# A fifth early group of attention weights, made by GpSimd as powers of two during the first MoE

## The chip, the cores and the metric

One core of one Trainium2 chip. The metric is the device time of one execution in microseconds (us), and lower is better. Each ratio below is the mean time of one kernel's fast runs over the mean of the fast runs of the kernel before in the same rounds on the same chip. It is therefore not quite the ratio of the medians that are quoted beside it.

## The reference

```python
def _attn_ref(q, kv, w_sr):            # q (4, 12288, 128), kv (4, 384, 32, 128)
    kv_pool = kv.reshape(B, H // 4, 4, W // 4, 4, C).mean(axis=(2, 4))
    k = v = kv_pool.reshape(B, -1, C) @ w_sr          # 768 keys a batch
    s = scale * (q @ k.transpose(0, 2, 1))
    a = np.exp(s - s.max(-1, keepdims=True))
    a /= a.sum(-1, keepdims=True) + 1e-09
    return a @ v
def _moe_ref(x, w_in, w_out):          # 49152 tokens, d_ff 2048
    h = x @ w_in
    return (h * (1.0 / (1.0 + np.exp(-1.702 * h)))) @ w_out
```

The attention's output is the MoE's input, token by token.

## The kernel before

Tokens are handled in 96 groups of 512. The first 48 pass through attention and then the MoE, and then the other 48 do the same. Per group, attention needs six chunks (128 keys x 512 queries) of exponentials and the MoE 16 chunks of the activation. A chunk is a matmul into PSUM, then a ScalarE activation into a ring of chunks in SBUF, then a second matmul that reads the ring. ScalarE takes three chunks in one instruction.

While the first MoE runs, VectorE has time to spare. The kernel lets it make the attention weights of four groups of the *second* attention ahead of time, as a polynomial of ten steps. They rest in reserved rows at the start of the ring.

```python
EARLY = 4
AG = 102                                   # chunks in the ring, reserved rows included
def early_exp(ps, out):                    # ten VectorE steps for one chunk
    nc.vector.tensor_scalar(a, ps, scale / LN2, -126.0, MUL, MAX)        # PSUM -> SBUF
    nc.vector.tensor_scalar(b, a, 127.0, MAGIC, MIN, ADD)                # SBUF -> SBUF
    nc.vector.tensor_scalar(e, b, MAGIC - 127.0, 2.0 ** 23, SUB, MUL)    # SBUF -> SBUF
    nc.vector.scalar_tensor_tensor(b, b, MAGIC, a, SUB, SUB)             # two SBUF inputs
    nc.vector.tensor_scalar_mul(a, b, COEFFS[5])                         # SBUF -> SBUF
    for k in (4, 3, 2, 1):
        nc.vector.scalar_tensor_tensor(a, a, COEFFS[k], b, ADD, MUL)     # two SBUF inputs
    nc.vector.scalar_tensor_tensor(out, a, COEFFS[0], e.bitcast(F32), ADD, MUL)
    # ... (yields between the steps cut)
```

The keys of batches 2 and 3 (counted from 0, so batch 3 is the fourth) are pooled by accumulating DMAs, issued from GpSimd's queue. A "gate" times those DMAs. It is a memset on VectorE followed by a memset of the same tile on GpSimd, so GpSimd issues no DMA before VectorE gets there.

```python
def gate():
    nc.vector.memset(gate_tile, 0.0)
    nc.gpsimd.memset(gate_tile, 0.0)
# ...
for b, lo in ((2, 2), (3, 24)):            # g: the group that the first MoE is at
    if lo <= g < lo + 8:
        gate()
        add_kv(b, g - lo)                  # two accumulating DMAs from GpSimd's queue
    if g in (lo + 10, lo + 12):
        use_kv(b, (g - lo - 10) // 2)      # VectorE adds the two halves, then keys and values
```

The softmax here doesn't subtract the row's maximum and nothing guards it: scores larger than these inputs give would overflow.

Of the kernel before, what the change touches and what calls it, by code (L numbers as in the profile page):

```python
# [7 lines left out]
F32 = mybir.dt.float32  # L8
# [6 lines left out]
MUL = mybir.AluOpType.mult  # L15
# [3 lines left out]
MAX = mybir.AluOpType.max  # L19
MIN = mybir.AluOpType.min  # L20
EQ = mybir.AluOpType.is_equal


@with_exitstack
def kernel(
    ctx, tc, q, kv, w_sr, moe_w_in, moe_w_out, out,
):
    nc = tc.nc
# [5 lines left out]
    JC = J // 128  # L34
    d_ff = moe_w_in.shape[1]
    FCH = d_ff // 128
    scale = 1.0 / (C ** 0.5)
    G = 512
# [3 lines left out]
    GB = NG // B  # L42
# [15 lines left out]

    R = 2
    XS = NS // R  # L60
    EARLY = 4
    AG = 102

    cpool = ctx.enter_context(tc.tile_pool(name="const", bufs=1))
    xpool = ctx.enter_context(tc.tile_pool(name="x", bufs=1))
# [5 lines left out]
    npool = ctx.enter_context(tc.tile_pool(name="norm", bufs=3))  # L71
# [9 lines left out]
    free = {6: 0.0, 7: 0.0}  # L81
    last_acc = 7

    def acc(key=None):

        nonlocal last_acc
        last_acc = next_acc()
        if key:
            closes[last_acc] = key
        return banks[:, last_acc, :]  # L90

    def next_acc():
        return min((m for m in (13 - last_acc, last_acc) if m not in closes), key=lambda m: free[m])
# [19 lines left out]
    kv_tiles, kv_sums, pooled, pTs, kTs, vs = {}, {}, {}, {}, {}, {}  # L113
# [83 lines left out]
    qTs = {}  # L197
# [58 lines left out]
    for m in range(0, 128, 32):  # L256
        p = slice(m, m + 32)
        nc.vector.tensor_tensor(ident[p, p], row[p], col[p], EQ)
        if m > 0:
# [16 lines left out]

    ag = agpool.tile([128, AG, 512], BF, name="ag")
    wide = cpool.tile([128, 16, 32], F32R)
# [12 lines left out]
    slot_of = {}  # L291
    head, low = 8 * JC, 0

    def place(chunks):
        nonlocal head
        if chunks[0][0] == "a" and chunks[0][1] < 8:
# [3 lines left out]
            return ag[:, lo[0]:lo[-1] + 1:JC, :]  # L300
        if head + len(chunks) > AG:
            head = low
# [9 lines left out]
    def room_ahead():  # L312
        busy = set(slot_of.values())
        return next((n for n in range(AG - low) if (head - low + n) % (AG - low) + low in busy), AG - low)

    early = range(NG // R, NG // R + EARLY)

    def weights(c):
        if c[0] == "a" and c[1] in early:
            return ag[:, (c[1] - early[0]) * JC + c[2], :]  # L320
        return ag[:, slot_of[c], :]
# [47 lines left out]
    LN2 = 0.6931471805599453  # L369
# [11 lines left out]
    def early_step():  # L381
        nonlocal steps
        on_dve(next(steps))
        if steps.gi_frame.f_locals["last"]:
            steps = None
            made.add(early_todo.pop(0))

    def early_exp(ps, out):
# [18 lines left out]
        last = True  # L407
        yield 3.5

    made = set()  # L410
    steps, early_todo = None, [(i, jc) for i in early for jc in range(JC)]

    def turn(w):

# [23 lines left out]
    av_of, xt_of, turns = {}, {}, []  # L438
# [33 lines left out]
    def background_moe(g):  # L472
# [7 lines left out]
        if g == 12:  # L480
            low = EARLY * JC
            head = max(head, low)
# [18 lines left out]
    extras = []  # L501
# [34 lines left out]
    seq, todo = [], []  # L536
    todo_early = [("a", t, a) for t in range(NT) for a in range(2) if (t // TS * TS + TS - 1) // 4 in early]
# [25 lines left out]
    def prepare(p):  # L563
# [10 lines left out]
        for i, _ in part:  # L574
# [25 lines left out]

    FIXED, CHUNK, SWITCH, HANDOVER, EVACUATE, LATE = 0.33, 1.975, 6.0, 1.0, 4.5, 1.0
    COST = {pool_chunk: (2.5, 2.0), key_chunk: (0.7, 2.0), value_chunk: (0.7, 2.0),
            transpose_q: (1.2, 4.0), early_fill: (1.0, 5.5), key_and_value: (1.0, 3.0),
            transpose_pooled: (1.5, 3.0), make_k: (1.0, 3.0), make_v: (1.5, 3.0), turn: (1.5, 3.5)}
    SMALL, TURN = 0.27, 5.5
    PAUSE = 4.0
    now, end, extra_at = 0.0, [], 0.0
    source, dve = None, 0.0

    def on_dve(cost):  # L610
        nonlocal dve
        dve = max(dve, now + 1.0) + cost


    def fill(p):
        nonlocal now
        if p >= len(seq):
            return
        kind, part = seq[p]
        prepare(p)  # L620
        lo = K * (p % 2)
        (fill_attn if kind == "a" else fill_moe)(part, banks[:, lo:lo + len(part), :])
        if p >= 2:
            now = max(now, end[p - 2] + HANDOVER / 2)
        now += len(part)
        begin = max(now + HANDOVER / 2, end[p - 1] if p else 0.0)
        if p and kind != seq[p - 1][0]:
            begin += SWITCH
        end.append(begin + FIXED + CHUNK * len(part))
# [3 lines left out]
    for n in range(len(seq)):  # L633
        fill(n + 2)
        while True:
            room = room_ahead()
            limit = end[-1] - K - HANDOVER if n + 3 < len(seq) else 1e9
            bank = free[next_acc()]
            f = None
            if turns and max(now, bank) >= turns[0][0]:  # L640
                f, args = turn, turns[0][1:]
            if f is None and extras and now >= max(extra_at, bank):
                f, *args = extras[0]
            if steps and dve <= now + 2.0:
                early_step()
            if not f and not steps and early_todo and low and min(slot_of.values()) >= low and (2, 1) in vs and dve <= now + 2.0 and now >= bank:
                f, args = early_fill, early_todo[0]
            if f and max(now, bank) + COST[f][0] > limit + (LATE if f is turn else 0.0 if f is early_fill else 4.5) and room >= 4 * K:
                f = None
            if f:  # L650
                now = max(now, bank) + COST[f][0]
                f(*args)
                free[last_acc] = dve + 1.0 if f is early_fill else now + COST[f][1]
                if f in (transpose_pooled, make_k, make_v):
                    on_dve(2.5)
                extra_at = max(now + PAUSE, dve + 1.5 if f in (transpose_pooled, make_k, make_v) else 0.0)
                if f is turn:
                    turns.pop(0)
                elif f is early_fill:
                    pass  # L660
                else:
                    extras.pop(0)
                continue
            if not source:

                if todo_early and all((i, jc) in made for t in range(todo_early[0][1], todo_early[0][1] + TS)
                                      for i in [t // 4] for jc in range(JC)):
                    source = todo_early
                else:
                    source = todo  # L670
            if not source:
                break
            kind, i, c = source[0]
            needs = at[("at" if kind == "a" else kind, i, c)]
            cost = K * SMALL if kind == "a" else 1.0
            first_of = c == 0 and (kind == "m" or i % TS == 0)
            if source is not todo_early and (needs > n or (kind == "a" and first_of and at["at", i + TS - 1, 1] > n)
                                             or (kind == "a" and i // 4 in early and (i // 4, JC - 1) not in made)):
                if first_of:
                    source = None  # L680
                break
            start = now if source is todo_early else max(now, end[needs] + HANDOVER)
            if first_of:
                start = max(start, bank)
            if start + cost > limit and not (room < 2 * K + 1 or (room < 4 * K and start == now)):
                if first_of:
                    source = None
                break
            now = start + cost
            (drain_attn if kind == "a" else drain_moe)(i, c)  # L690
            source.pop(0)
            if not todo_early:
                low = 0
            if c == (1 if kind == "a" else FCH - 1) and (kind == "m" or i % TS == TS - 1):
                source = None
    assert not todo and not todo_early and not turns and not extras and not early_todo


# [28 lines left out]
```

## Time and profile before

| | before |
|---|---|
| time | 971.72 us median of 3 (971.57 to 972.06) |
| span of the profiled run | 969.9 us, granted TensorE clock 0.999 |
| TensorE / ScalarE busy | 947.4 / 946.2 us |
| VectorE / GpSimd busy | 344.3 / 66.1 us |
| first MoE, from the 10th group on (255 to 490 us) | TensorE 233.4, ScalarE 232.3, VectorE 173.0, GpSimd 22.5 of 235 us |

Three rows of the page's slices are added here. The span is cut into 40 equal slices, and a digit is the busy share of a slice in tenths.

```profile
PE   7899999999999999999999999999999999999997
...
POOL 3100100330000242000000000000000000000000
PEclk9999999999999999999999999999999999999999
```

TensorE is busy for 90% or more of every slice from the third to the last but one. GpSimd (POOL) is nearly empty, and that emptiness is what the change wants to use.

### The profile page before, as it was taken

To read this page: it belongs to the slowest core of one execution; us is meant where nothing else is said; L and a number is where in the kernel's file an instruction comes from. 1 tells how busy PE (TensorE), PEld (TensorE's weight loads), DVE (VectorE), ACT (ScalarE), POOL (GpSimd) and SP (SyncE) were. 2 spreads that over 40 slices of the span, in tenths; PEclk is the share of its full clock that TensorE was granted. 3 is DMA by queue.
4 is the path that set the end of the run, shared out by engine and by line. 5 is a ranking of instruction groups with operands and counts; after the bars stand their busy time and mean duration, and the time that the engine had idled before them with its cause. 6 is when DMAs were issued, how large, how long until landed. Compare 5 with 4: busy or idle time off the path is not lost.

```text
span 969.9 us, 15710 instructions
## 1 busy us (share of the span) xinstructions
PE 947.4 (98%) x6243; PEld 508.4 (52%) x6359; DVE 344.3 (35%) x734; ACT 946.2 (98%) x705; POOL 66.1 (7%) x113
## 2 busy tenths in 40 slices
PE   7899999999999999999999999999999999999997
PEld 3567777644444444454445777754444444444443
DVE  4444333211578778778312333320110110101010
ACT  4999999999999999999999999999999999999997
POOL 3100100330000242000000000000000000000000
PEclk9999999999999999999999999999999999999999
DMA  9897861999852799224429976562222222222222
GB/s 182 161 196 150 113 96 34 109 159 171 173 107 33 102 155 113 40 36 78 77 44 155 193 142 121 110 131 43 44 33 44 44 33 44 40 37 40 37 33 44
DMA packets 354169, 89.70 MB, mean 92 GB/s; under 512 B 328048, under 2 KB 351728, under 8 KB 353776
## 3 DMA queue, kind: packets, MB, share of 16 engines
q1 hardware_dynamic: 323936, 56.06, 34.2%
q0 software_dynamic: 29104, 32.51, 21.9%
q8 instruction: 49, 0.80, 0.3%
q10 hardware_dynamic: 1056, 0.13, 0.1%
q14 instruction: 24, 0.20, 0.1%
HBM read 52.49 MB, written 45.88 MB: 101 GB/s over the span
## 4 chain that ended last, share of the span: by engine, by line
PE 80%; ACT 16%; issue 2%; DVE 1%; DMA 1%; POOL 0%; POOLq 0%
PE banks L515 27%; PE banks L508 26%; ACT ag L510 14%; PE banks L340 14%; PE banks L329 11%; ACT ag L331 2%; DVE qT L230 1%; DMA x<-in_kv_dram 1%; PE banks L377 1%; PE banks L419 0%; PE banks L134 0%; PE banks L224 0%; DVE xt L357 0%; PE banks L271 0%; DVE o_sb L523 0%
## 5 line engine op out<-in xcount | busy, mean ns | idle before, releaser
L510 ACT ACTIVATE ag<-banks 128x1536 bf16<-128x1536 f32 x512 | 691.1, 1512 | 2.9 <-PE banks L508 2.2
L515 PE MATMUL banks<-ag,w_out_sb 128*128 128x512 bf16 x1523 | 410.1, 379 | 2.9 <-ACT ag L510 0.5
L508 PE MATMUL banks<-x,w_in_sb 128*128 128x512 bf16 x1478 | 406.0, 378 | 2.0 <-ACT ag L510 0.4
L331 ACT ACTIVATE ag<-banks 128x1536 bf16<-128x1536 f32 (+1 forms) x188 | 249.4, 1481 | 11.2 <-PE banks L329 10.8
L515 PEld LDWEIGHTS <-w_out_sb 128*128 128x128 bf16 x1536 | 149.8, 98 | 179.9 <-issue 1.0
L508 PEld LDWEIGHTS <-w_in_sb 128*128 128x128 bf16 x1536 | 147.8, 97 | 174.0 <-issue 14.1
L523 DVE STREAM_TRANSPOSE o_sb<-banks 128x512 f32<-128x512 f32 x96 | 68.7, 716 | 395.6 <-PE banks L515 372.6
L340 PEld LDWEIGHTS <-ag 128*128 128x128 bf16 x2304 | 149.9, 97 | 48.1 <-issue 1.6
L340 PE MATMUL banks<-v,ag 128*128 128x129 bf16 x2304 | 167.9, 220 | 0.7 <-DVE v L158 0.7
L329 PE MATMUL banks<-qT,kT 128*128 128x512 bf16 x507 | 146.3, 378 | 8.0 <-ACT ag L331 4.5
L349 DVE RECIPROCAL rec<-banks 128x3 f32<-128x3 f32 x128 | 23.0, 180 | 139.0 <-PE banks L340 138.9
L404 DVE SCALAR_TENSOR_TENSOR ea<-ea,eb 128x512 f32<-128x512 f32 x96 | 66.0, 687 | 2.8
L329 PEld LDWEIGHTS <-kT 128*128 128x128 bf16 x552 | 47.3, 97 | 34.6 <-issue 4.2
L357 DVE TENSOR_TENSOR x<-banks,rec 128x384 bf16<-128x384 f32 x104 | 57.9, 557 | 3.6
L166 POOL DMA_DIRECT2D kvs<-in_kv_dram x32 | 40.6, 1319 | 27.9 <-DMA kvs<-in_kv_dram 25.5
L444 POOL MEMSET gate_tile<- 1x8 f32 x38 | 3.8, 100 | 450.1 <-DVE gate_tile L443 450.1
L393 DVE TENSOR_SCALAR ea<-banks 128x512 f32<-128x512 f32 x24 | 16.6, 691 | 26.5 <-PE banks L377 26.5
L406 DVE SCALAR_TENSOR_TENSOR ag<-ea,ee 128x512 bf16<-128x512 f32 x24 | 16.5, 689 | 1.1
L399 DVE SCALAR_TENSOR_TENSOR eb<-eb,ea 128x512 f32<-128x512 f32 x24 | 16.5, 687 | 0.7
L357 DVE TENSOR_TENSOR xt<-banks,rec 128x384 bf16<-128x384 f32 x24 | 13.4, 557 | 0.8
L230 DVE COPY qT<-banks 128x512 bf16<-128x512 bf16 x15 | 9.8, 687 | 4.5 <-PE banks L224 4.4
L421 DVE COPY x<-banks 128x768 bf16<-128x768 bf16 x12 | 6.7, 557 | 11.7 <-PE banks L419 11.7
(65 smaller groups left out, 154.8 us busy)
## 6 DMA issues: line engine op xcount, KB each, us to landing
out_dram<-o_sb SPq DMA_DIRECT2D x382, 64.0 KB, 2.0
kvs<-in_kv_dram POOLq DMA_DIRECT2D x32, 384.0 KB, 6.4
q_bf<-in_q_dram POOLq DMA_DIRECT2D x20, 512.0 KB, 6.8
x_bf<-x SPq DMA_DIRECT2D x13, 768.0 KB, 5.6
x<-in_kv_dram POOLq DMA_DIRECT2D x12, 512.0 KB, 12.5
x<-in_q_dram POOLq DMA_DIRECT2D x3, 512.0 KB, 20.0
w_in_sb<-in_moe_w_in_dram POOLq DMA_DIRECT2D x1, 512.0 KB, 5.0
w_out_sb<-in_moe_w_out_dram POOLq DMA_DIRECT2D x1, 512.0 KB, 7.2
```

Source lines behind the costliest of these rows:

```text
L166: nc.gpsimd.dma_start(out=kv_sums[b][:, i2], in_=kv_p[b, i, w, :, i2], **({"accum_op": ADD} if n else {}))
L230: nc.vector.tensor_copy(dst, src)
L329: nc.tensor.matmul(ps[:, k, :], kTs[i // GB][:, jc * 128:(jc + 1) * 128], rhs, start=True, stop=True)
L331: nc.scalar.activation(place([("a",) + c for c in chunks]), ps, AF.Exp, scale=scale)
L340: nc.tensor.matmul(av_of[u][:, k * (C + 1):(k + 1) * (C + 1)], weights(("a", i, jc))[:, o:o + T], vs[i // GB][:, jc, 0:C + 1], start=(jc = ...
L349: nc.vector.reciprocal(rec, ps[:, :, C])
L357: nc.vector.tensor_tensor(to, ps[:, :, 0:C], rec.unsqueeze(2).broadcast_to([128, TS, C]), MUL)
L404: nc.vector.scalar_tensor_tensor(a, a, COEFFS[k], b, ADD, MUL)
L508: nc.tensor.matmul(ps[:, k, :], w_in_sb[:, fc * 128:(fc + 1) * 128], x[:, g % (4 * XS) * G:(g % (4 * XS) + 1) * G], start=True, stop=True)
L510: nc.scalar.activation(place([("m",) + c for c in chunks]), ps, AF.Gelu_apprx_sigmoid)
L515: nc.tensor.matmul(o_of[g], w_out_sb[:, fc, :], weights(("m", g, fc)), start=(fc == 0), stop=(fc == FCH - 1))
L523: nc.vector.transpose(o_sb, o_of.pop(g))
```

## The change

A fifth group's six chunks are made early too. TensorE writes the scores of a chunk to PSUM, VectorE scales them to y, and GpSimd computes 2 to the power y straight into the ring. In the second attention ScalarE then has six chunks of exponentials fewer. y has two buffers. The ring has 99 chunks in place of 102, and 30 of them are reserved in place of 24. In the kernel's own order planning a power costs POWER = 150 units.

```diff
-    EARLY = 4
-    AG = 102
+    EARLY = 5
+    BY_DVE = 4
+    AG = 99
# ...
+    def pow_fill(i, jc):
+        nonlocal pool
+        ps = acc()
+        rhs = qTs[i // 4][:, 0, (i % 4) * G:(i % 4 + 1) * G]
+        nc.tensor.matmul(ps, kTs[i // GB][:, jc * 128:(jc + 1) * 128], rhs, start=True, stop=True)
+        y = npool.tile([128, 512], F32, name="y", bufs=2)
+        nc.vector.tensor_scalar(y, ps, scale / LN2, 127.0, MUL, MIN)
+        on_dve(3.5)
+        nc.gpsimd.tensor_tensor(weights(("a", i, jc)), two.broadcast_to([128, 512]), y, POW)
+        pool = max(pool, dve) + POWER
+        made.add(pow_todo.pop(0))
# ...
+    POWER = 150.0
# ...
+            if not f and pow_todo and low and min(slot_of.values()) >= low and (2, 1) in vs and pool <= now and dve <= now + 4.0 and now >= bank:
+                f, args = pow_fill, pow_todo[0]
# ... (the lists of chunks to make and small edits to the planner cut)
```

More of the change, by code (lines that the diff above doesn't have):

```diff
@@ L21 @@
 EQ = mybir.AluOpType.is_equal
+POW = mybir.AluOpType.pow
 @with_exitstack
@@ L408, in early_exp @@
         yield 3.5
+    two = cpool.tile([128, 1], F32)
+    nc.vector.memset(two, 2.0)
+    def pow_fill(i, jc):
[9 more added lines that the diff above has]
+        made.add(pow_todo.pop(0))
     made = set()
-    steps, early_todo = None, [(i, jc) for i in early for jc in range(JC)]
+    steps, early_todo = None, [(i, jc) for i in early[:BY_DVE] for jc in range(JC)]
+    pow_todo = [(i, jc) for i in early[BY_DVE:] for jc in range(JC)]
     def turn(w):
@@ L602 @@
     COST = {pool_chunk: (2.5, 2.0), key_chunk: (0.7, 2.0), value_chunk: (0.7, 2.0),
-            transpose_q: (1.2, 4.0), early_fill: (1.0, 5.5), key_and_value: (1.0, 3.0),
+            transpose_q: (1.2, 4.0), early_fill: (1.0, 5.5), pow_fill: (1.0, 5.5), key_and_value: (1.0, 3.0),
             transpose_pooled: (1.5, 3.0), make_k: (1.0, 3.0), make_v: (1.5, 3.0), turn: (1.5, 3.5)}
@@ L607 @@
     now, end, extra_at = 0.0, [], 0.0
-    source, dve = None, 0.0
+    source, dve, pool = None, 0.0, 0.0
+    POWER = 150.0
     def on_dve(cost):
@@ L643 @@
                 f, *args = extras[0]
-            if steps and dve <= now + 2.0:
+            if not f and pow_todo and low and min(slot_of.values()) >= low and (2, 1) in vs and pool <= now and dve <= now + 4.0 and now >= bank:
+                f, args = pow_fill, pow_todo[0]
+            if steps and dve <= now + 2.0 and f is not pow_fill:
                 early_step()
@@ L652 @@
                 f(*args)
-                free[last_acc] = dve + 1.0 if f is early_fill else now + COST[f][1]
+                free[last_acc] = dve + 1.0 if f in (early_fill, pow_fill) else now + COST[f][1]
                 if f in (transpose_pooled, make_k, make_v):
@@ L658 @@
                     turns.pop(0)
-                elif f is early_fill:
+                elif f in (early_fill, pow_fill):
                     pass
@@ L695 @@
                 source = None
-    assert not todo and not todo_early and not turns and not extras and not early_todo
+    assert not todo and not todo_early and not turns and not extras and not early_todo and not pow_todo
 _INS = ['q', 'kv', 'w_sr', 'moe_w_in', 'moe_w_out']
```

## The prediction

> **What bounds the kernel now.** I read the page's busy shares first, then the chain of work that ended last, then the groups of instructions, and last the order of time inside the first MoE, where the new work goes.
>
> ```profile
> PE 947.4 (98%) x6243; PEld 508.4 (52%) x6359; DVE 344.3 (35%) x734; ACT 946.2 (98%) x705; POOL 66.1 (7%) x113
> PE 80%; ACT 16%; issue 2%; DVE 1%; DMA 1%; POOL 0%; POOLq 0%
> ```
>
> TensorE and ScalarE are both busy for 98% of 969.9 us, and the chain passes between these two only. So work taken from ScalarE alone buys at most what ScalarE did, and less where TensorE is the one that ends last; and any stop of TensorE is paid almost in full, because neither of the two has room to catch up.
>
> ```profile
> L510 ACT ACTIVATE ag<-banks 128x1536 bf16<-128x1536 f32 x512 | 691.1, 1512 | 2.9 <-PE banks L508 2.2
> L331 ACT ACTIVATE ag<-banks 128x1536 bf16<-128x1536 f32 (+1 forms) x188 | 249.4, 1481 | 11.2 <-PE banks L329 10.8
> L523 DVE STREAM_TRANSPOSE o_sb<-banks 128x512 f32<-128x512 f32 x96 | 68.7, 716 | 395.6 <-PE banks L515 372.6
> L393 DVE TENSOR_SCALAR ea<-banks 128x512 f32<-128x512 f32 x24 | 16.6, 691 | 26.5 <-PE banks L377 26.5
> L401 DVE TENSOR_SCALAR ea<-eb 128x512 f32<-128x512 f32 x24 | 10.3, 431 | 0.6
> L404 DVE SCALAR_TENSOR_TENSOR ea<-ea,eb 128x512 f32<-128x512 f32 x96 | 66.0, 687 | 2.8
> L444 POOL MEMSET gate_tile<- 1x8 f32 x38 | 3.8, 100 | 450.1 <-DVE gate_tile L443 450.1
> ```
>
> Read here: busy time of ScalarE is 691.1 / 512 = 1.35 us for three chunks, so 0.45 us a chunk. VectorE empties a PSUM bank of every MoE group with one transpose (0.72 us); it also makes 24 chunks of exponentials by ten polynomial steps each. Of these ten, three (scalar operand, SBUF to SBUF) take about 0.43 us, one (from PSUM) 0.69 us, and six (two tensors from SBUF) 0.69 us. GpSimd does nothing that reads SBUF: it issues DMAs, and waits for VectorE's little gate memset.
>
> The stretch that the change enters, in order of time:
>
> ```profile
> 315.14 0.72 DVE L523 STREAM_TRANSPOSE o_sb<-banks 128x512 f32<-128x512 f32 x1 [0.69 <-PE banks L515]
> 316.86 0.69 DVE L393 TENSOR_SCALAR ea<-banks 128x512 f32<-128x512 f32 x1 [1.01 <-PE banks L377]
> 317.59 0.43 DVE L395 TENSOR_SCALAR eb<-ea 128x512 f32<-128x512 f32 x1
> ...
> 321.05 0.07 DVE L443 MEMSET gate_tile<- 1x8 f32 x1
> ...
> 322.04 0.72 DVE L523 STREAM_TRANSPOSE o_sb<-banks 128x512 f32<-128x512 f32 x1 [0.21 <-PE banks L515]
> ...
> 328.21 0.07 DVE L443 MEMSET gate_tile<- 1x8 f32 x1
> ```
>
> One MoE group takes about 7 us (transposes at 315.14 and 322.04). The polynomial fills nearly all the time between: VectorE is busy 93.9 of the 120 us from 300 to 420. It runs in order, so whatever holds one step holds the next transpose, and with it one of the only two PSUM banks that TensorE accumulates in.
>
> **What the Trainium skill says.** "SBUF — State Buffer", section "SBUF: two separate sides": VectorE's second pair of SBUF ports is shared with GpSimd; it "is an exclusive lock, not a bandwidth split", the one that starts first has it for its whole instruction and the other blocks; it concerns VectorE instructions in a two-port mode and those with two SBUF inputs (the latter against a GpSimd instruction that reads SBUF). "VectorE: DVE Perf Modes", section "Mode 2×_2P": a single-source fp32 instruction between SBUF and SBUF uses both ports and gives two elements per cycle. The trace agrees with the second: 0.43 us against 0.69 us from PSUM. So nine of the ten steps want the shared pair. The lock itself no instruction of the kernel before can show. "GPSIMD Engine Reference", section "Performance versus the Vector engine", gives an add of two 2048-wide fp32 tensors 4,497 ns on GpSimd; no page that I found gives pow. "TensorE: Matmul & The Clock Gate", section "What's actually happening": after an idle window of about 3.4 us the array runs at half clock until it has been busy for another. The trace before has no such pause (granted clock 0.999).
>
> **The change part by part.**
>
> Removed: six chunks of Exp in the second attention, two activations of three: 6 x 0.45 = 2.7 us of ScalarE. With TensorE as loaded as ScalarE, I expect 1 to 2.7 us of it, at most 0.3% of the time.
>
> Moved: six score matmuls (about 0.215 us each, as three in a row start every 0.65 us) go from the second attention into the first MoE. Net on TensorE: nothing.
>
> Added on VectorE: six times y = score x factor from PSUM, like the 0.69 us of the row L393: 4.1 us, beside other work.
>
> Added on GpSimd: six pow over 128x512. The trace before has no pow. The kernel's own plan gives it 150 of its units; three chunks of ScalarE are 0.33 + 3 x 1.975 = 6.255 units in that plan and take 1.35 us, so a unit is 0.216 us and a pow is planned at 32 us. Six are 194 us; they fit into the MoE for GpSimd's own time. As the figure looks like a measured one with some margin, I take 28 us (an estimate, 15 to 40).
>
> What they hold up is the point. In the built order the six y stand after the 10th, 15th, 20th, 25th, 29th and 34th group's transpose, all inside the polynomial's 24 chunks (from before the 12th to after the 41st transpose). After y the first step that wants the shared pair is next or at most two instructions off. If the lock holds, VectorE stands until the pow ends. TensorE then goes on until it meets a matmul into a bank not yet emptied. I counted its matmuls in the built order, from the one that feeds y to that point, at 0.215 us for 512 columns: 9.9, 3.9, 7.8, 7.7, 7.3 and 6.2 us, mean 7.1 (no allowance for its own waits). Against that stand about 1.1 us until y starts (26.5 / 24 in row L393), 0.7 us of y, the pow, and some 2 us of steps until the transpose that frees the bank. So each pow stops TensorE for P + 4 - 7 = P - 3 us. With P = 28: 25 us, six times 150 us. ScalarE starves with it, since its fills stand behind the blocked matmul in TensorE's order. Restarting at half clock costs about 1.7 us each, 10 in all. Sum: 972 + 150 + 10 - 2 = 1,130 us. With P = 20 it is some 1,080, with P = 35 some 1,172.
>
> The ring (99 chunks, of which 30 instead of 24 are set aside: 69 instead of 78) gives up nine chunks, or three activations, of slack. ScalarE waits almost nowhere, so I give this 0 to 2 us. The library load that the build puts ahead of the first pow delays GpSimd only.
>
> **The rivals.** (1) No lock of that length, but the gate. Each gate is a memset on VectorE and then one on GpSimd of the same tile; the next VectorE memset waits for GpSimd's last, as the built program's semaphores say. Today it costs nothing, since GpSimd is always there first (its memset follows VectorE's by 0.1 us). In the changed order one gate stands right after the third y and one right after the fourth, each followed by a second gate about 5 to 8 us later. GpSimd reaches the first of each pair only after its pow, so VectorE stands at the second: P - 7 less about 7 of TensorE's tolerance, 14 us at P = 28, twice, plus the accumulating loads of the fourth batch's keys, which run 6.4 us each and get late for their sum (the 31st group): perhaps 5 more. That makes about 972 + 33 = 1,005 us. For it: it needs no rule of the chip beyond the semaphores. Against it as the main term: it works twice, the lock six times; under the lock it is the same wait, and not added.
>
> (2) Everything is hidden. GpSimd is 7% busy, VectorE 35%, the pow is short (under 12 us) or does not lock, and the time falls by up to 2.7 us: 969 to 972. For it: whoever wrote it spaced the pow generously and lets VectorE be nearly free before each. Against it: the gate order above, which alone spoils it unless P is under some 15 us.
>
> (3) The pow is much slower than planned, say 60 us. Then six stops of 57 us give 1,320, and the third y waits for its buffer as well. The spacing of the plan speaks against it; I give it one in twelve.
>
> **Range and chances.** I give the lock 0.72, the gate alone 0.14, the hidden case 0.14. Under the lock the spread is that of P: 1,060 to 1,190. I put the point a little under that case's 1,130, as the other cases all lie below: 1,110 us, with 985 to 1,190 as the range. Faster by over 2% can't be: the whole saving is 0.3%. Within 2% is the hidden case and a corner of the gate case. The rest is slower.
>
> **What would show it.** Under the lock, the row of one of VectorE's two-input or two-port steps shows single instructions of 10 to 30 us (or idle time of the same length before them), six in number, each ending with a pow; TensorE and ScalarE show six holes of 20 to 30 us between the 10th and 41st group, and the page's slices of the first MoE drop from 9 to 5 to 7 in both rows. TensorE's clock falls below 1 there. After the first MoE the second half should look as before, minus two activations. If instead the holes are two and VectorE waits at the gate memset for GpSimd, rival 1 is right. If VectorE's steps keep their 0.43 and 0.69 us while a pow runs, the lock is refuted here. A pow of under 10 us, or one of over 40, makes the size wrong with the mechanism standing.

## The result

| | before | after |
|---|---|---|
| time, median | 971.64 us (4 runs) | 1292.74 us (4 runs) |
| ratio | | 1.3304 (95%: 1.3285 to 1.3323) |
| span of the profiled run | 969.9 us | 1290.7 us |
| TensorE / ScalarE busy | 947.4 / 946.2 us | 958.7 / 944.4 us |
| GpSimd busy | 66.1 us | 557.0 us |
| mean granted TensorE clock | 0.999 | 0.878 |

The change costs 33%, and the output is correct. From the page of the kernel after, the shares, the slices, the chain that ended last and the row of the power:

```profile
PE 958.7 (74%) x6242; PEld 510.9 (40%) x6359; DVE 349.4 (27%) x741; ACT 944.4 (73%) x703; POOL 557.0 (43%) x119
...
PE   7999999999400004800899501999999999999998
...
POOL 2100032099999997799599998000000000000000
PEclk9999999999755556955899855999999999999999
...
PE 42%; issue 20%; POOL 19%; ACT 15%; DVE 2%; DMA 2%; DVEq 0%; ACTq 0%; POOLq 0%
...
L423 POOL TENSOR_TENSOR ag<-two,y 128x512 bf16<-128x512 f32 x6 | 492.1, 82026 | 49.1 <-DVE y L421 49.1
```

The last row holds the main fact. One power over 128x512 takes 82.0 us, and six take 492 us. TensorE's row has three holes, and GpSimd is busy through each of them. The work of TensorE and ScalarE hardly changed, so the extra time is waiting.

The list of waits of the kernel after says who waited for whom, with the total in us, the number of times and the longest:

```profile
DVE gate_tile L461 <- POOL gate_tile L462: 157.8, 1, 157.8
PE banks L533 <- DVE ea L395: 153.9, 1, 153.9
...
DVE eb L401 <- issue: 74.4, 1, 74.4
PE banks L379 <- DVE o_sb L541: 72.5, 1, 72.5
...
PE banks L342 <- POOL gate_tile L462: 72.3, 1, 72.3
...
DVE y L421 <- POOL ag L423: 15.5, 1, 15.5
...
PE banks L533 <- DVE y L421: 10.3, 1, 10.3
```

Each TensorE hole pairs with something that stands behind powers in GpSimd's queue. The order of time on VectorE shows this (start and duration in us; the brackets hold the idle time before and what ended it):

```profile
337.58 0.69 DVE L421 TENSOR_SCALAR y<-banks 128x512 f32<-128x512 f32 x1 [15.46 <-POOL ag L423]
...
339.06 0.07 DVE L461 MEMSET gate_tile<- 1x8 f32 x1
...
501.46 0.07 DVE L461 MEMSET gate_tile<- 1x8 f32 x1 [157.78 <-POOL gate_tile L462]
...
613.51 0.68 DVE L401 SCALAR_TENSOR_TENSOR eb<-eb,ea 128x512 f32<-128x512 f32 x1 [74.44 <-issue]
613.52 0.07 DVE L461 MEMSET gate_tile<- 1x8 f32 x1
...
802.46 0.18 DVE L351 RECIPROCAL rec<-banks 128x3 f32<-128x3 f32 x1 [73.08 <-PE banks L342]
```

1. The third y waits 15.5 us for a buffer, until the first power ends.
2. The gate at 339.06 follows the third y. Its GpSimd half stands behind the second and third powers, which end at 501.3. The next gate's VectorE half must wait for that, so VectorE stands for 157.8 us.
3. The records of the fourth power and of GpSimd's gate memset behind it both end at 613.4, and VectorE goes on at 613.5. The profile calls this wait "issue". The step that waits has two SBUF inputs, so by itself this trace leaves the predicted port lock as a rival here. The run gates below settles it. Only the gate is freed there. The gate memset stands in front of the same step, and the step runs without a wait, although a power runs beside it (the third, 419.4 to 501.3 us in that run):

```profile
430.88 0.06 DVE L463 MEMSET gate_tile<- 1x1 f32 x1
430.97 0.69 DVE L401 SCALAR_TENSOR_TENSOR eb<-eb,ea 128x512 f32<-128x512 f32 x1
```

4. The sixth power ends at 801.4, and at 801.48 TensorE starts the matmul that needs its weights. The profile names the GpSimd gate memset as releaser, which is GpSimd's next small event. Two of the experiments (gates and loads_first) name the power itself.

The four VectorE waits add up to 15.5 + 157.8 + 74.4 + 73.1 = 320.8 us. The span grew by 1290.7 - 969.9 = 320.8 us. Before and after the waits the two kernels agree. The output transposes of VectorE, one per MoE group, come within 3.3 us of each other up to the 20th group, and from the 43rd group to the last the kernel after is 318 to 321 us late.

The exact match of the sums is partly luck, since TensorE's own stops are 1 to 5 us shorter than these waits. They are 10.3 + 153.9 + 72.5 + 72.3 = 309.0 us. After them it ran at half its clock for 6.0, 5.9, 2.9 and 3.6 us by the trace's clock records, 18.4 us in all. An estimated half of that, 9 us, is lost, which makes 318 of the 321 us.

The wait that was predicted does not occur. The next fence shows VectorE's steps inside the first power, which runs from 255.6 to 337.5 us:

```profile
257.42 0.43 DVE L397 TENSOR_SCALAR eb<-ea 128x512 f32<-128x512 f32 x1
257.88 0.43 DVE L399 TENSOR_SCALAR ee<-eb 128x512 int32<-128x512 f32 x1
258.34 0.69 DVE L401 SCALAR_TENSOR_TENSOR eb<-eb,ea 128x512 f32<-128x512 f32 x1
```

Two-port steps keep 0.43 us and two-input steps 0.69 us beside the power. Of the 158 such steps that lie inside the six powers, 157 keep their length. The other one took 0.93 us, and it began 0.7 us after the second power did. One more, at 530.8 us, was running when the fourth power and a DMA issue of GpSimd began, and it took 2.35 us. So a short hold at the start of a power is possible, but none of the whole power.

### The profile page after: what moved, and what is told of

Same layout as the page of the kernel before. It is cut to its first block, busy times and chain, and to the rows that moved or that the text cites. A ratio compares the mean times of both kernels' runs of the same rounds, so it can differ in the third digit from the quotient of the medians.

```text
span 1290.7 us, 15727 instructions
## 1 busy us (share of the span) xinstructions
PE 958.7 (74%) x6242; PEld 510.9 (40%) x6359; DVE 349.4 (27%) x741; ACT 944.4 (73%) x703; POOL 557.0 (43%) x119
## 4 chain that ended last, share of the span: by engine, by line
PE 42%; issue 20%; POOL 19%; ACT 15%; DVE 2%; DMA 2%; DVEq 0%; ACTq 0%; POOLq 0%
POOL ag L423 19%; ACT ag L528 13%; PE banks L526 12%; PE banks L533 12%; PE banks L342 9%; PE banks L331 8%; DMA qT<-q_bf 2%; ACT ag L333 1%; DVE ea L406 1%; DVE qT L232 1%; PE banks L273 0%; DVE y L421 0%; PE banks L226 0%; PE banks L437 0%; DVE eb L401 0%
## 5 line engine op out<-in xcount | busy, mean ns | idle before, releaser
L533 PE MATMUL banks<-ag,w_out_sb 128*128 128x512 bf16 x1505 | 412.2, 382 | 166.6 <-DVE ea L395 153.9
L423 POOL TENSOR_TENSOR ag<-two,y 128x512 bf16<-128x512 f32 x6 | 492.1, 82026 | 49.1 <-DVE y L421 49.1
L526 PE MATMUL banks<-x,w_in_sb 128*128 128x512 bf16 x1493 | 414.7, 381 | 2.4
L333 ACT ACTIVATE ag<-banks 128x1536 bf16<-128x1536 f32 (+1 forms) x186 | 246.6, 1443 | 10.8 <-PE banks L331 10.4
L342 PE MATMUL banks<-v,ag 128*128 128x129 bf16 x2304 | 167.6, 220 | 74.1 <-POOL gate_tile L462 72.3
L331 PE MATMUL banks<-qT,kT 128*128 128x512 bf16 x503 | 145.3, 378 | 8.2 <-ACT ag L333 4.5
L462 POOL MEMSET gate_tile<- 1x8 f32 x38 | 7.7, 203 | 223.4 <-DVE gate_tile L461 223.4
L379 PE MATMUL banks<-qT,kT 128*128 128x512 bf16 x24 | 9.6, 398 | 72.5 <-DVE o_sb L541 72.5
L461 DVE MEMSET gate_tile<- 1x8 f32 x38 | 2.5, 65 | 157.8 <-POOL gate_tile L462 157.8
L401 DVE SCALAR_TENSOR_TENSOR eb<-eb,ea 128x512 f32<-128x512 f32 x24 | 16.8, 700 | 75.2 <-issue 74.4
L395 DVE TENSOR_SCALAR ea<-banks 128x512 f32<-128x512 f32 x24 | 16.6, 692 | 26.2 <-PE banks L379 26.1
```

Source lines behind the costliest of these rows:

```text
L331: nc.tensor.matmul(ps[:, k, :], kTs[i // GB][:, jc * 128:(jc + 1) * 128], rhs, start=True, stop=True)
L333: nc.scalar.activation(place([("a",) + c for c in chunks]), ps, AF.Exp, scale=scale)
L342: nc.tensor.matmul(av_of[u][:, k * (C + 1):(k + 1) * (C + 1)], weights(("a", i, jc))[:, o:o + T], vs[i // GB][:, jc, 0:C + 1], start=(jc = ...
L423: nc.gpsimd.tensor_tensor(weights(("a", i, jc)), two.broadcast_to([128, 512]), y, POW)
L526: nc.tensor.matmul(ps[:, k, :], w_in_sb[:, fc * 128:(fc + 1) * 128], x[:, g % (4 * XS) * G:(g % (4 * XS) + 1) * G], start=True, stop=True)
L533: nc.tensor.matmul(o_of[g], w_out_sb[:, fc, :], weights(("m", g, fc)), start=(fc == 0), stop=(fc == FCH - 1))
```

## The experiments

All ran beside the kernel before. "Wrong on purpose" means that the edit spoils the weights of one group and leaves the order of instructions alone (loads_first also moves loads and powers, and mult30_gates adds products).

| run | edit to | what it changes | median us | ratio (95%) |
|---|---|---|---|---|
| mult | after | power becomes product, 1.06 us | 974.27 | 1.0016 (1.0004 to 1.0029) |
| pow64 | after | power of 64 columns, 10.8 us | 983.91 | 1.0122 (1.0108 to 1.0135) |
| pow192 | after | power of 192 columns, 31.2 us | 1023.40 | 1.0528 (1.0514 to 1.0542) |
| gates | after | gate on eight columns in turn | 1282.63 | 1.3191 (1.3173 to 1.3209) |
| pow192_gates | after | both | 1018.46 | 1.0477 (1.0456 to 1.0499) |
| loads_first | pow192_gates | last key loads before the powers | 1005.27 | 1.0354 (1.0326 to 1.0381) |
| mult30_gates | gates | thirty products for each power | 1075.19 | 1.1054 (1.1038 to 1.1071) |
| dve5 | after | fifth group by VectorE too, no power | 973.28 | 1.0007 (0.9993 to 1.0021) |
| ring96 | before | ring 96 | 972.58 | 1.0005 (0.9992 to 1.0019) |
| ring93 | before | ring 93 | 973.80 | 1.0017 (1.0004 to 1.0029) |

### mult: all but the duration

```diff
-        nc.gpsimd.tensor_tensor(weights(("a", i, jc)), two.broadcast_to([128, 512]), y, POW)
+        nc.gpsimd.tensor_tensor(weights(("a", i, jc)), two.broadcast_to([128, 512]), y, MUL)
```

> The changed kernel with the six powers made plain products (wrong result on purpose): same queues, same order, same gates, only the duration of GpSimd's six instructions falls from 82 us to an estimated 1 to 2 us. Theory (the 82 us behind which GpSimd's own queue, the gates and the last weights wait are the whole loss): 968 to 973 us, no VectorE wait over 8 us in the first MoE. Rival (the smaller ring, the sixth row of reserved slots or the new steps on VectorE cost something of their own): over 980 us.

Wrong. The median was 974.27 us, the ratio is 1.0016, and the time is 1 us over the expected band. In the profile a product takes 1.06 us (median), and VectorE has no long wait. Practically the whole loss is therefore due to the length of the six powers. The new order, ring, steps and library load together cost 0.16%, and no gain is left.

### pow192: powers as long as the plan allows

```diff
-        nc.gpsimd.tensor_tensor(weights(("a", i, jc)), two.broadcast_to([128, 512]), y, POW)
+        w = weights(("a", i, jc))
+        nc.gpsimd.tensor_tensor(w[:, 0:192], two.broadcast_to([128, 192]), y[:, 0:192], POW)
+        nc.gpsimd.tensor_tensor(w[:, 192:512], two.broadcast_to([128, 320]), y[:, 192:512], MUL)
```

> The changed kernel with the power taken of 192 of the 512 columns only and a plain product for the rest (wrong result on purpose), so that GpSimd needs an estimated 31 us for a chunk (192/512 of 82), about what the kernel's plan allows it. Theory (queue and gates, no lock): two waits of VectorE at a gate memset for GpSimd of about 25 us each, TensorE stopped for some 18 us in each, a smaller wait for the last keys, 1000 to 1025 us. Rival (what was predicted, a lock of the SBUF ports for the whole power): six stops, 1110 to 1160 us. If the plan's figure had been enough: 968 to 975 us.

Wrong. The time was 1023.4 us, inside the band that the theory of queue and gates expected. VectorE's two long waits, in order of time:

```profile
355.74 0.07 DVE L463 MEMSET gate_tile<- 1x8 f32 x1 [26.38 <-POOL gate_tile L464]
...
418.13 0.68 DVE L401 SCALAR_TENSOR_TENSOR eb<-eb,ea 128x512 f32<-128x512 f32 x1 [26.12 <-issue]
```

Together they are 52.5 us, and the ratio is 1.0528, or 51 us. TensorE stopped for 21.7 and 23.8 us of them, more than the 18 that I expected, and no wait for the last keys is listed. The predicted lock would have made six stops. So even with a power of 31 us, close to the predicted 28, the time would not have been the predicted 1,110 to 1,130.

### pow64: a power short enough to hide?

The edit is that of pow192 with 64 columns.

> Powers of 64 columns, an estimated 11 us with the product of the rest (64/512 of 82, and 0.9), the gates as in the changed kernel (wrong result on purpose). Theory (a gate wait is the power's length less the 5.7 us from its scores to the second gate, of which TensorE swallows about 2): two waits of about 5 us, 975 to 982 us. Rival (each power costs in proportion to its length, 320/82 us per us over the six): 1005 to 1020 us.

Wrong. The median was 983.9 us, a little over the theory's band and far from the proportional rival. The powers take 10.8 us, and the two gate waits are 6.2 and 7.3 us. TensorE stopped for 1.5 and 5.0 us, so it swallowed 4.7 and 2.3 us of them, as in pow192. Half clock for 4.7 us after the second stop adds an estimated 2.3 us, and mult shows 1.6 us without any long wait. That makes 10.4 of the 12 us by which this run is longer than the kernel before; the rest stays open. That the sum of the two gate waits, 13.5 us, is close to 12 too is chance.

### gates: free the gate, keep the powers

```diff
-        nc.vector.memset(gate_tile, 0.0)
-        nc.gpsimd.memset(gate_tile, 0.0)
# ... (gates, a counter, cut)
+        n = next(gates) % 8
+        nc.vector.memset(gate_tile[:, n:n + 1], 0.0)
+        nc.gpsimd.memset(gate_tile[:, n:n + 1], 0.0)
```

> The changed kernel, powers of full width, but the gate's memsets go round eight columns of the tile, so that VectorE no longer waits for GpSimd's memset before. Theory (GpSimd's queue itself is the bound, the gate is only where VectorE meets it): the waits of 158 and 74 us at the gate go, but the sum of the last keys takes their place, since its loads stand behind the same powers; GpSimd stays busy without a pause from the first power on; 1260 to 1295 us. Rival (the gate is the cause): both waits vanish, 1040 to 1090 us.

The result is correct. The time was 1282.63 us, as the theory expected, and only 10 us better than the kernel after. The gate waits are gone from the list of waits. Instead the sum of the last keys (pooled) waits for loads, y for a free buffer, and TensorE for the sixth power:

```profile
DVE pooled L174 <- DMA kvs<-in_kv_dram: 125.5, 1, 125.5
...
DVE y L421 <- POOL ag L423: 112.9, 3, 49.5
...
PE banks L342 <- POOL ag L423: 70.0, 1, 70.0
```

GpSimd works from 255.6 to 790.3 us without a long pause. At this length of power its queue is the bound. The gate is only one of the places where the other engines meet that queue.

### pow192_gates and loads_first: one wait after another

> Powers of 192 columns (31.2 us each, as measured) and the gate's memsets on eight columns in turn (wrong result on purpose). Theory (at this length GpSimd is not the bound, so the two waits of 26 us at the gate are the whole loss of 50 us): no VectorE wait for GpSimd, the last keys' sum waits for its loads some 0 to 15 us instead, 972 to 988 us. Rival (the powers cost time in another way, by their ports or by late keys): over 1000 us.

Wrong. The theory missed: 1018.46 us, where I expected 972 to 988. The gate waits had gone, but the loads of the last keys still stand behind the first three powers, and some of them behind the fourth as well:

```profile
DVE pooled L174 <- DMA kvs<-in_kv_dram: 43.8, 1, 43.8
```

In pow192 this wait had been hidden by the gate waits before it. The next run also takes the loads away from behind the powers:

```diff
-        for b, lo in ((2, 2), (3, 24)):
+        for b, lo in ((2, 2), (3, 15)):
# ... and a power starts only once (3, 1) in vs, where it was (2, 1) in vs
```

> Powers of 192 columns, gates on eight columns in turn, and the loads of the fourth batch's keys put ahead of all six powers in GpSimd's queue (they begin with the 15th group in place of the 24th; a power starts only once those keys are made; wrong result on purpose). Theory (the 46 us that stayed when the gate was freed are the key loads standing behind three powers): no wait of VectorE for these loads over 5 us, 972 to 982 us. Rival (powers of 31 us cost time wherever they stand): over 1000 us.

Wrong. Half of the theory held: the wait for the loads is gone (none is listed), and TensorE runs the whole first MoE without a hole. But the powers now start about 100 us later, and the sixth ends at 555.5 us, while TensorE needs it at about 527:

```profile
PE banks L342 <- POOL ag L424: 29.1, 1, 29.1
```

That wait is most of the 33 us over the kernel before. Freeing one dependence of the queue exposed the next, twice.

### mult30_gates: the port lock by itself

```diff
-        nc.gpsimd.tensor_tensor(weights(("a", i, jc)), two.broadcast_to([128, 512]), y, POW)
+        for _ in range(30):
+            nc.gpsimd.tensor_tensor(weights(("a", i, jc)), two.broadcast_to([128, 512]), y, MUL)
```

> In place of each power thirty plain products in a row, of the same two operands (1.06 us each as measured, so 32 us of GpSimd reading two SBUF inputs nearly without a pause), gates on eight columns in turn (wrong result on purpose). It measures the port lock by itself. Theory A (the lock is real, but a power rarely holds the ports because it computes far more than it reads): VectorE's steps with two SBUF inputs or in the two-port mode become longer than 0.69 and 0.43 us beside the products, by up to one product (1 us) each, and the products stretch too; 975 to 1010 us. Theory B (no lock in these forms): steps of VectorE keep 0.69 and 0.43 us, 972 to 988 us as the powers of 192 columns with the same gates.

Wrong. The time was 1075.19 us, longer than even Theory A allowed, and 57 us longer than pow192_gates, where GpSimd is busy for 32 us for each chunk against 37 to 41 us here. VectorE's busy time grew from 350.0 us there to 431.5. Its steps beside the products, in order of time:

```profile
256.54 0.69 DVE L395 TENSOR_SCALAR ea<-banks 128x512 f32<-128x512 f32 x1 [0.63 <-PE banks L379]
...
257.91 1.15 DVE L399 TENSOR_SCALAR ee<-eb 128x512 int32<-128x512 f32 x1
259.09 1.41 DVE L401 SCALAR_TENSOR_TENSOR eb<-eb,ea 128x512 f32<-128x512 f32 x1
260.53 1.15 DVE L403 TENSOR_SCALAR ea<-eb 128x512 f32<-128x512 f32 x1
```

Most two-input steps go from 0.69 to 1.41 us, and two of the three two-port steps (L399, L403) from 0.43 to 1.15 us, each 0.72 us longer. The third (L397), which follows the step that reads PSUM, mostly keeps 0.43 us. The products stretch from 1.06 to 1.245 us on the mean. The step that reads PSUM (L395) is the control: it keeps 0.69 us beside the products every time. So what the products hold up is the steps that want the shared ports, and not VectorE as a whole. The two engines exclude each other with plain products, and with a power they do not, although the same two operands, of the same shape and types, are read in both cases.

### dve5, ring96 and ring93: what the fifth group is worth, and the ring

```diff
-    BY_DVE = 4
-    AG = 99
+    BY_DVE = 5
+    AG = 101
```

> Five early groups, all by VectorE's polynomial (30 chunks), no power and no GpSimd work; ring of 101 chunks. This asks what the fifth group is worth when its making is hidden. Theory: ScalarE loses two Exp activations (2.7 us) and TensorE nothing, so 968.5 to 971.5 us, a gain of 0 to 0.3%. Rival (VectorE can't make six more chunks in time, or the smaller ring starves): 973 to 990 us.

Correct, ratio 1.0007, the same time; the median of 973.28 us is over the theory's band and at the edge of the rival's. ScalarE's busy time falls as intended, from 946.2 to 944.3 us, while TensorE's hardly moves (947.4 and 946.6 us), and TensorE is the longer of the two. So the fifth group gains nothing measurable even when its making is hidden. A shorter ring might have taken back what ScalarE saved, which is why I tried it alone on the kernel before (AG = 96, AG = 93).

> The kernel before with its ring cut from 102 to 96 chunks (72 beside the 24 reserved ones). With 93 chunks the time rose by 0.17%, but the result was wrong without being meant to be. Theory (a smaller ring costs a little): correct, ratio 1.0003 to 1.002. Rival (the ring has slack, 93 chunks was a case of its own): ratio within 0.0005 of 1.

Correct, ratio 1.0005 with an interval from 0.9992 to 1.0019. The ratio lies in both expected bands, so the run decides nothing between them. A cost of the ring of up to 0.19% isn't excluded, and the saving that was hoped for is 0.28% (2.7 us).

> The kernel before with its ring cut from 102 to 93 chunks, so that 69 are left beside the 24 reserved ones, as in the changed kernel. Theory (the ring has slack to spare): 971 to 973 us, ratio within 0.1%. Rival (the ring is what took back the 2.7 us of ScalarE when the fifth group's making was hidden): 973.5 to 977 us.

Ratio 1.0017 and 973.80 us, in the rival's band, but this kernel's result was wrong without being meant to be, for a reason that I did not find, so it carries little. Whether the ring's nine chunks explain the 0.16% of mult, or the missing gain of dve5, stays open.

## Why the prediction was wrong

The direction was right (slower). The time was 1292.7 us, far outside 985 to 1190. The step that failed is "So each pow stops TensorE for P + 4 - 7 = P - 3 us", six times, by the port lock. In its place, VectorE waited at a buffer and at two gates, and TensorE for the last power (15.5, 157.8, 74.4 and 73.1 us), and each power was 2.9 times as long as assumed. The length alone does not mend it: with P = 82 the prediction's own sum would be 972 + 6 x 79 + 10 - 2 = 1,454 us.

- **What was removed**: predicted as 1 to 2.7 us of gain. ScalarE did lose most of that (dve5: 1.9 us of busy time), but no gain in time could be measured.
- **What the powers hold up**: "If the lock holds, VectorE stands until the pow ends" failed as a mechanism. Beside a power the steps keep 0.43 and 0.69 us. The same lock is real with plain products, which mult30_gates shows. So the statement of the Trainium skill ("SBUF — State Buffer", section "SBUF: two separate sides") was good for one instruction of GpSimd and not for the other.
- **Length of a power**: this is the term that was mis-sized most. "I take 28 us (an estimate, 15 to 40)" came from the plan's constant of 150 units, "as the figure looks like a measured one with some margin". It measured 82.0 us. The third rival had 60 us at one in twelve, with 1,320 us. That this lies near 1292.7 is luck, since it comes from six stops by the lock.
- **The first rival, the gate**, was the mechanism of the two longest waits, and at 31 us it is nearly the whole loss (pow192: 52.5 us of waits against 51 us). Its wait of VectorE, "P - 7", is 25 us at 32 us, and 26.4 and 26.1 were measured. What it had wrong is "about 7 of TensorE's tolerance": TensorE swallowed 4.7 and 2.3 us of the two waits. It did run on for 5.5 and 6.3 us after VectorE stopped, but it started again only 0.8 and 4.0 us after VectorE did. Such a lag was counted under the lock ("some 2 us of steps") and left out here.
- **"The third y waits for its buffer as well"**, said under the third rival, came true (15.5 us). **Late keys**, put at "perhaps 5 more", are 43.8 us once the gate no longer hides them.
- **Missed altogether**: the planner marks a power's chunk as made when it is issued, and "Six are 194 us; they fit into the MoE for GpSimd's own time" hid the check of the far end. TensorE waited 72.3 us for the sixth power. With powers of 31 us in the same order (pow192) it does not wait there.
- **The slower clock** after each stop came as said, and longer: half clock for 2.9 to 6.0 us, so an estimated 1.5 to 3.0 us lost each time, where the prediction's estimate was 1.7. On the mean the granted clock was 0.878.

What is shown: the length of the powers causes practically all of the loss (mult), and it acts through GpSimd's queue at four meeting points: a buffer of y, the gates, the loads of the last keys and the last weights. What stays open: why a power does not keep the SBUF ports. No run looks inside the instruction.

## What to carry to other kernels

Before putting a new operation on an idle engine, measure its length by itself. An author's planning constant is not a measurement, and 512 columns of power took 82 us where 1.06 us made a product. Then list everything that stands behind it in that engine's queue (semaphores back to a busy engine, DMA issues, the last consumer) and ask when each is due. Freeing only the first of these shows the next. And ask first what the work is worth if it were free: here the fifth group, made by VectorE, gained nothing measurable. TensorE carries the same load as ScalarE, which is the likely reason but is not shown apart from the smaller ring.

## What the Trainium skill lacked or had wrong

- "SBUF — State Buffer", section "SBUF: two separate sides", has either side keep the shared ports for its whole instruction. With GpSimd's products this agrees (VectorE's 0.43 us became 1.15, its 0.69 us became 1.41). With GpSimd's power it does not: inside the six powers of 82 us, 157 of 158 such steps kept their length.
- "GPSIMD Engine Reference", section "Performance versus the Vector engine", has an add of 2048 columns at 4,497 ns. An estimate from that, a quarter or 1.1 us, fits the product of 512 columns here (1.06 us). Neither this page nor any other that I found has pow: 10.8 us for 64 columns, 31.2 us for 192 and 82.0 us for 512, about 0.16 us a column.
- No page that I found says what a gate between two engines costs once the far engine gets long work: each wait at a gate here was what GpSimd still had queued in front of it, less 5 to 8 us (26.4 us for 32 us, 74.4 us for 82 us, 157.8 us for two powers of 82 us).
